# mLSTM cell and leaky-ReLU feed-forward on one core: w_in's row blocks over both partition halves, and row tiles that swap PSUM banks at a drain

## The chip, the core and the metric

The kernel runs on one core of a Trainium2 chip. The core has five engines that work at the same time, each from its own queue of instructions in a fixed order: TensorE (PE in the profile; its weight loads are PEld), VectorE (DVE), ScalarE (ACT), GpSimd (POOL) and SyncE (SP, which here only issues DMAs). Matrix products read SBUF and leave their results in PSUM[...]. The metric is the device time of one execution in microseconds, lower is better; three executions of the kernel before gave 541.49, 541.57 and 542.69.

## The reference

An mLSTM cell runs over 4 batches, 8 heads, 768 time steps and heads of 40; its output, 3072 tokens of 320, goes through a feed-forward layer of width 2048 with a leaky ReLU.

```python
for t in range(S):
    m_new = np.maximum(f_gate[:, :, t] + m, i_gate[:, :, t])
    f_stab = np.exp(f_gate[:, :, t] + m - m_new)
    i_stab = np.exp(i_gate[:, :, t] - m_new)
    C = f_stab * C + i_stab * einsum('bhd,bhe->bhde', v_t, k_t)
    n = f_stab * n + i_stab * k_t
    y_t = sigmoid(o_t) * einsum('bhde,bhe->bhd', C, q_t) / maximum(abs(sum(n * q_t)), 1)
x = y.transpose(0, 2, 1, 3).reshape(3072, 320)
h = x @ w_in                      # 320 x 2048
out = np.maximum(0.01 * h, h) @ w_out   # 2048 x 320
```

All activations are float32. The two weight matrices come as float64; the kernel reads them as 64-bit words and narrows them to float32 itself.

## The kernel before

**Chunks and steps.** The 768 time steps are cut into six chunks of 128. A step s is one batch of one chunk (s = 4 * chunk + batch), so there are 24. The cell's work of a step is two pieces: `u_parts` (the products of keys, queries and values, and the state's increments, L576 and L581) and then `u_plain` (chunk 1, L629) or `u_mix` (chunks 2 to 5, L659), which make x of that step. The texts below call them parts(s), plain(s) and mix(s). Between them `ahead(s + 1)` prepares the next step: copies on ACT, products on DVE, and on POOL the values `vu` (L458), the state (L556) and the mask (L429); for steps up to 7 it also holds `u_split`, transposes on TensorE with four ACT copies after them (L504). The mask's exponentials (L437, ACT) are handed out three per unit of feed-forward work. Chunk 0 has code of its own, `first_chunk`.

**Feed-forward groups.** Group g is the feed-forward work on the 512 tokens of chunk g; it runs while the cell works on chunk g + 1. It has 32 units. Units 0 to 15 are the first product (`ph`, L723) with a relu on ACT (L731): 320 rows of w_in are five row blocks of 64, and a matmul takes one block of 64 rows on one half of the partitions, so that two row tiles of TensorE, r = 0 (partitions 0 to 63) and r = 1 (64 to 127), work side by side. A pair j is two FF tiles of 128, one for each row tile: row tile r always writes PSUM bank `ph[r]`, and each half of the partitions holds all five blocks of its own tiles, in the order `SLOTS[r]`. A pair has ten matmuls of 512 columns, cut into a unit of six and a unit of four, after which two relus empty the two banks. Four banks (`psf`, tag `mm`) hold two pairs, so that one is emptied while the next fills. Group 0 works in halves of 256 columns, ten matmuls to a unit. Units 16 to 31 are the second product (`po`, L758), 4 matmuls each; each is 128 x 128 by 128 x 320.

**x.** The first product reads x transposed, `xT`, as five blocks of 64 rows on either half. In chunks 0 and 1, `u_x` makes it: three transposes to PSUM and five ACT copies (L709 to L713). Later mix(s) writes x to DRAM, and `gather_x` reads it back with four DMAs.

**Weights.** `load_weights(n)` brings w_in's four column blocks (n < 4; ten DMAs of 64 rows x 256 words each, L213) and w_out's eight row blocks (L218). `narrow_weights(n)` turns one into float32, with one ACT operation (L231) and six DVE operations (L233 to L247). Blocks 0 and 1 are narrowed in the first chunk, the other ten step by step in group 0's units: two steps in units up to 9, then three, from 14 on four.

**Order.** TensorE, DVE, ACT and POOL keep the order in which the program calls them; SP's DMAs are placed by the tile framework. The last loop is that order: unit i of the feed-forward, then any cell pieces due after it. In chunk 1 `place` names the units after which the 13 pieces come; in later chunks the nine pieces (eight in the last) are spread evenly over the first 24 units, which puts them after units 2, 5, 7, 10, 13, 15, 18, 21 and 23. The gates of the next chunk follow unit 0 (DVE) and unit 2 (ACT, L294 and L295); its transposes (L310, L315) are one of the nine pieces. When chunk 5 is done, group 5 runs with no cell pieces.

Of the kernel before, what the change touches and what calls it, by code (L numbers as in the profile page):

```python
# [9 lines left out]
F32 = mybir.dt.float32  # L10
U32 = mybir.dt.uint32
U64 = mybir.dt.uint64
AF = mybir.ActivationFunctionType
# [5 lines left out]
def kernel(  # L19
# [26 lines left out]
    nc = tc.nc  # L46
# [22 lines left out]
    SLOTS = ([0, 2, 4, 1, 3], [1, 3, 0, 2, 4])  # L69
    assert NB * P == S and NF * P == FF and NF % 4 == 0 and D <= DP and H == 2 * PR and BH <= P  # L70
    assert KR == DP and KC == 5 and KC * DP == Dm and GT * 4 <= 2048
# [96 lines left out]
    def f_of(r, j):  # L168
        n, e = divmod(j, 2)
        return 4 * n + 2 * r + e  # L170

    def w_row(r, slot, j):
        n, e = divmod(j, 2)
        at = (2 * slot + e) * P
        return w_in[DP * r : DP * (r + 1), n, at : at + P]

    def run_of(r, at):

        ks = SLOTS[r][at:]
        return ks[0], next((i for i in range(1, len(ks)) if ks[i] != ks[i - 1] + 2), len(ks))  # L180
# [7 lines left out]
    def load_weights(n):  # L188
# [20 lines left out]
        if n < QN:  # L209
            src = moe_w_in[:, n * QC : (n + 1) * QC].rearrange("(k p) (r c) -> r p k c", p=DP, r=2)  # L210
            for slot in range(KC):
                for r in range(2):
                    nc.sync.dma_start(  # L213
                        to[DP * r : DP * (r + 1), 2 * P * slot : 2 * P * (slot + 1)], src[r, :, SLOTS[r][slot], :],
                    )
        else:
            rows = moe_w_out[2 * m * P : 2 * (m + 1) * P, :]
            nc.sync.dma_start(to.rearrange("p (a d) -> p a d", d=Dm), rows.rearrange("(a p) d -> p a d", p=P))  # L218
# [464 lines left out]
    def gather_x(s):  # L683

        c, b = divmod(s, B)
        if ("xT", c) not in st:
            st["xT", c] = wk.tile([P, KC, GT], F32, name="xT", bufs=1)
        xT = st["xT", c]
        src = x_dr[s].rearrange("(k p) t -> p k t", p=DP)
        for r in range(2):  # L690
            at = 0
            while at < KC:
                k0, n = run_of(r, at)
                nc.sync.dma_start(xT[DP * r : DP * (r + 1), at : at + n, ts(b, P)], src[:, k0 : k0 + 2 * n - 1 : 2, :])
                at += n

    def u_x(s):

        c, b = divmod(s, B)
        d = st[s]  # L700
        if b == 0:
            st["xT", c] = wk.tile([P, KC, GT], F32, name="xT", bufs=1)
        xT = st["xT", c]
        xt = psc.tile([P, KF + 1, P], F32, name="xt", tag="c")
        for kk in range(KF):
            nc.tensor.transpose(xt[:, kk, :], d["x"][:, ts(kk, P)], ident[:])
        nc.tensor.transpose(xt[:KR, KF, :], d["x"][:, KF * P :], ident[:])
        tok = ts(b, P)
        nc.scalar.copy(xT[:, :KF, tok], xt[:, :KF, :])  # L709
        nc.scalar.copy(xT[:DP, KF + 1 :, tok], xt[DP:, :KF, :])  # L710
        nc.scalar.copy(xT[DP:, KF : 2 * KF, tok], xt[:DP, :KF, :])
        nc.scalar.copy(xT[:DP, KF, tok], xt[:DP, KF, :])
        nc.scalar.copy(xT[DP:, 2 * KF, tok], xt[:DP, KF, :])  # L713
        del st[s]


    def ff_units(g):
        xT = st["xT", g]

        def rows(j, ph, cols, slots):  # L720
            for slot in slots:
                for r in range(2):
                    nc.tensor.matmul(  # L723
                        ph[r][:, cols], lhsT=w_row(r, slot, j), rhs=xT[DP * r : DP * (r + 1), slot, cols],
                        start=(slot == 0), stop=(slot == KC - 1),
                    )

        def relu(j, ph, cols):
            for r in range(2):
                f = f_of(r, j)  # L730
                nc.scalar.activation(acts[:, f, cols], ph[r][:, cols], AF.Prelu, alpha=0.01)  # L731

        def pair(j):
            ph = []

            def first():
                ph.extend(psf.tile([P, GT], F32, name=f"ph{r}", tag="mm") for r in range(2))
                rows(j, ph, slice(0, GT), range(3))

            def second():  # L740
                rows(j, ph, slice(0, GT), range(3, KC))
                relu(j, ph, slice(0, GT))

            return [first, second]

        def half(j, h):
            ph = [psf.tile([P, GT], F32, name=f"ph{r}", tag="mm") for r in range(2)]
            cols = ts(h, GT // 2)
            rows(j, ph, cols, range(KC))
            relu(j, ph, cols)  # L750
# [18 lines left out]
        if g == 0:  # L769

            ins = [(j, h) for j0 in range(0, NF // 2, 2) for h in range(2) for j in (j0, j0 + 1)]
            return [lambda j=j, h=h: half(j, h) for j, h in ins] + [
                lambda n=n, m=m: part(n, m) for m in range(4) for n in range(B)
            ]
        return [u for j in range(NF // 2) for u in pair(j)] + [
# [118 lines left out]
    with tc.manual_schedule(engines={E.PE, E.DVE, E.Activation, E.Pool}):  # L894
# [16 lines left out]
        place = (2, 5, 7, 10, 12, 15, 16, 18, 21, 22, 24, 26, 28)  # L911
        now = (None for n in range(2, QN + NF // 2) for _ in narrow_weights(n))
        for c in range(1, NB + 1):
# [6 lines left out]
            for i in range(n_ff):  # L920
# [16 lines left out]
                upto = sum(p <= i for p in place) if c == 1 else min(n_c, (i + 1) * n_c // (n_ff - 8))  # L937
# [50 lines left out]
```

## Time and profile before

| | us |
|---|---|
| three executions, median (lowest to highest) | 541.57 (541.49 to 542.69) |
| the profiled execution | 542.91 |
| its span, first to last instruction | 541.1 |
| TensorE busy | 523.1 (97%) |
| first product on TensorE (L723), 1120 records | 218.9 |
| second product on TensorE (L758), 768 records | 216.2 |
| VectorE busy | 249.8 (46%) |
| ScalarE busy | 163.3 (30%) |
| GpSimd busy | 120.4 (22%) |
| mean granted clock of TensorE | 0.962 |

A float32 matmul shows as two records. Idle time of an engine that is not the bound costs nothing, and a wait is named by the engine that released it last. The chain of work that ended last lies on TensorE for 86% of the span. The page also has the span in 40 slices of 13.5 us, with the busy share in tenths.

### The profile page before, as it was taken

The page shows a single profiled execution, that of the slowest core. Times are in us where ns is not written, and L with a number is a line of the kernel's source. Part 1 is how long each engine was busy: PE and PEld are TensorE (multiplying, and loading weights), DVE is VectorE, ACT ScalarE, POOL GpSimd, SP SyncE. Part 2 cuts the span into 40 slices and gives each one's busy share as a digit, 9 for nine tenths or more (in the row PEclk, how much of TensorE's full clock was granted, in tenths as well). Part 3 has the DMA queues.
Part 4 walks back from the last instruction along what each step waited for, and adds up shares of the span by engine and source line. Part 5 has one row for each costly group of instructions (what it writes and reads, how often), then busy time and mean ns, then how long its engine had stood idle before and what let it go on. Part 6 is the DMA issues. An engine that isn't in the chain of part 4 may idle for free.

```text
span 541.1 us, 11162 instructions
## 1 busy us (share of the span) xinstructions
PE 523.1 (97%) x4372; PEld 339.3 (63%) x4372; DVE 249.8 (46%) x443; ACT 163.3 (30%) x450; POOL 120.4 (22%) x157
## 2 busy tenths in 40 slices
PE   7989969979999999999999999999999999999997
PEld 7877858756745477645577645567654577644675
DVE  4688896999635536135527135625034532000000
ACT  4566653533433320034220043310043400022100
POOL 4134352252303332103333003423002100000000
PEclk9658988979999999999999999999999999999999
DMA  9976687977525555564655554556531121100000
GB/s 116 165 202 150 158 202 196 185 169 145 129 68 105 124 139 128 135 130 92 128 144 129 143 121 98 129 142 141 123 100 51 50 84 34 42 1 0 13 12 24
DMA packets 166003, 60.18 MB, mean 111 GB/s; under 512 B 129024, under 2 KB 156224, under 8 KB 165952
## 3 DMA queue, kind: packets, MB, share of 16 engines
q1 hardware_dynamic: 165568, 59.35, 49.6%
q8 instruction: 34, 0.56, 0.4%
q10 hardware_dynamic: 384, 0.13, 0.1%
q14 instruction: 17, 0.14, 0.1%
HBM read 52.72 MB, written 6.72 MB: 110 GB/s over the span
## 4 chain that ended last, share of the span: by engine, by line
PE 86%; DVE 6%; DMA 3%; SPq 2%; ACT 1%; issue 1%; POOL 1%; DVEq 0%; POOLq 0%; ACTq 0%
PE ph L723 37%; PE po L758 36%; PE pT L659 3%; PE sd L576 3%; DMA S<-in_v_dram 1%; PE warm L305 1%; PE sd L581 1%; PE pa L604 1%; DMA raw<-in_moe_w_out_dram 1%; PE sc L524 1%; ACT w L437 1%; PE ab L416 1%; POOL vu L458 1%; PE tkq L512 1%; DVE qn L586 1%
## 5 line engine op out<-in xcount | busy, mean ns | idle before, releaser
L723 PE MATMUL ph<-xT,w_in 64*128 64x512 f32 (+1 forms) x1120 | 218.9, 542 | 0.1
L758 PE MATMUL po<-w_out,acts 128*128 128x320 f32 x768 | 216.2, 440 | 0.0
L758 PEld LDWEIGHTS po<-w_out,acts 128*128 128x128 f32 x768 | 145.8, 193 | 60.7 <-issue 4.0
L723 PEld LDWEIGHTS ph<-xT,w_in 64*128 64x128 f32 x1120 | 108.4, 191 | 91.0 <-issue 84.2
L731 ACT ACTIVATE acts<-ph 128x512 f32<-128x512 f32 (+1 forms) x112 | 54.0, 534 | 153.6 <-PE ph L723 153.5
L586 DVE TENSOR_TENSOR qn<-w,sd 64x512 f32<-64x512 f32 x40 | 27.4, 685 | 122.7 <-PE sd L581 87.8
L556 POOL TENSOR_TENSOR S<-S,f 40x336 f32<-40x336 f32 x36 | 28.8, 800 | 181.3 <-PE pT L659 135.9
L437 ACT ACTIVATE w<-w,gT 128x64 f32<-128x64 f32 (+1 forms) x192 | 52.4, 350 | 1.0 <-DVE w L423 1.0
L484 DVE TENSOR_TENSOR qn<-kqT,ea 64x512 f32<-64x512 f32 (+1 forms) x40 | 30.2, 755 | 4.7 <-ACT kqT L504 3.4
L458 POOL TENSOR_TENSOR vu<-S,gT 64x336 f32<-64x336 f32 x36 | 31.4, 871 | 2.7
L673 POOL TENSOR_TENSOR xb<-xb,den 128x320 f32<-128x320 f32 x16 | 11.6, 727 | 88.5 <-DVE xb L670 88.5
L766 ACT COPY y<-po 128x320 f32<-128x320 f32 x12 | 5.1, 425 | 86.7 <-PE po L758 86.7
L766 ACT COPY hn<-po 128x320 f32<-128x320 f32 x12 | 5.1, 425 | 86.3 <-PE po L758 86.3
L576 PEld LDWEIGHTS sd<-kqT 40*64 40x64 f32 x640 | 21.1, 138 | 12.8 <-issue 10.5
L666 DVE STREAM_TRANSPOSE hb<-pT 128x512 f32<-128x512 f32 x16 | 11.5, 717 | 38.1 <-PE pT L659 38.1
L429 POOL TENSOR_TENSOR w<-w,i 128x512 f32<-128x512 f32 x20 | 27.3, 1365 | 7.9 <-ACT acts L731 6.5
L581 PE MATMUL sd<-vu,kn 64*40 64x42 f32 x576 | 21.2, 218 | 4.0 <-POOL vu L458 4.0
L576 PE MATMUL sd<-kqT 40*64 40x64 f32 x640 | 24.2, 225 | 0.4 <-DVE S L560 0.2
L659 PEld LDWEIGHTS pT<-qn,S 128*64 128x64 f32 x512 | 16.2, 138 | 10.5 <-issue 6.9
L581 PEld LDWEIGHTS sd<-vu,kn 64*40 64x40 f32 x576 | 18.6, 114 | 4.2 <-POOL vu L458 4.2
L677 DVE STREAM_TRANSPOSE x<-xb 128x512 f32<-128x512 f32 x16 | 17.7, 1104 | 7.8 <-POOL xb L673 7.8
L478 DVE STREAM_TRANSPOSE kqT<-rb 128x512 f32<-128x512 f32 x32 | 20.6, 680 | 0.0
(123 smaller groups left out, 362.4 us busy)
## 6 DMA issues: line engine op xcount, KB each, us to landing
w<-a_dr SPq DMA_DIRECT2D x40, 128.0 KB
ea<-a_dr SPq DMA_DIRECT2D x40, 128.0 KB
rb<-in_k_dram SPq DMA_DIRECT2D x64, 80.0 KB
rb<-in_q_dram SPq DMA_DIRECT2D x64, 80.0 KB
rb<-in_o_gate_dram SPq DMA_DIRECT2D x64, 80.0 KB
kn<-in_k_dram SPq DMA_DIRECT2D x24, 160.0 KB
raw<-in_moe_w_out_dram SPq DMA_DIRECT2D x6, 640.0 KB
S<-in_v_dram SPq DMA_DIRECT2D x80, 40.0 KB
```

Source lines behind the costliest of these rows:

```text
L429: nc.gpsimd.tensor_tensor(w, w, cm2.unsqueeze(1).to_broadcast([P, H, SL]), op=ALU.add)
L437: yield nc.scalar.activation(w[:, h, :], w[:, h, :], AF.Exp, bias=gT[c][:, 0, bh : bh + 1], scale=1.0)
L458: nc.gpsimd.tensor_tensor(d["vu"][rows], S_v[s % NL][rows, u, :, :, :V1], g[rows].to_broadcast([SL, H, 2, V1]), op=ALU.mult,)
L484: nc.vector.tensor_tensor(mixed(s)[rows, 1 - r], d["kqT"][rows, 1].rearrange("p (h t) -> p h t", t=SL), d["ea"][rows], op=ALU.mult,)
L556: nc.gpsimd.tensor_tensor(new, old, g, op=ALU.mult)
L576: nc.tensor.matmul(bank[1 - u][toks, h, :], lhsT=kqT[rows, 0, ts(h, SL)], rhs=kqT[rows, 1, ts(h, SL)], start=True, stop=True,)
L581: nc.tensor.matmul(dC[u][:, h].rearrange("p k d -> p (k d)"), lhsT=d["k"][toks, h, :D], rhs=d["vu"][toks, h].rearrange("p k d -> p (k d)") ...
L586: nc.vector.tensor_tensor(mixed(s)[toks, u], w[toks], bank[1 - u][toks], op=ALU.mult)
L659: nc.tensor.matmul(pT[DP * r : DP * (r + 1), j * P + u * SL : j * P + (u + 1) * SL], lhsT=S[:, u, h, :], rhs=m[:, u, h, :], start=True, st ...
L723: nc.tensor.matmul(ph[r][:, cols], lhsT=w_row(r, slot, j), rhs=xT[DP * r : DP * (r + 1), slot, cols], start=(slot == 0), stop=(slot == KC ...
L731: nc.scalar.activation(acts[:, f, cols], ph[r][:, cols], AF.Prelu, alpha=0.01)
L758: nc.tensor.matmul(po[n][:], lhsT=acts[:, f, ts(n, P)], rhs=w_out[:, f, :], start=(f == 0), stop=(f == NF - 1),)
```

## The change

w_in is laid out anew: of its five row blocks of 64, blocks 0 and 2 lie on partitions 0 to 63, blocks 1 and 3 on 64 to 127, once for all FF tiles, and block 4 on the upper half for the first two FF tiles of a column block and on the lower for the other two. One DMA brings the first four row blocks, two more bring the fifth: three for a column block, not ten. xT has three places, not five: rows 0 to 127, rows 128 to 255, and the last 64 rows on both halves. `u_x` makes it with four transposes and one ACT copy, `gather_x` with three DMAs.

So one FF tile's sum now takes products from both row tiles, in turn. Four FF tiles make a group of four units and hold four PSUM banks: `head(0)` and `head(1)` open two banks each, with the blocks of one row tile for each bank; then TensorE drains (`nc.tensor.drain()`), and `tail(0)` and `tail(1)` finish them with the row tiles swapped over the banks, each followed by two relus, the later bank first. A head has four matmuls, a tail six. Group 0, in halves of 256 columns, has both heads in one unit and both tails in the next.

The cell's pieces are placed so that they come between heads and tails where they fall in the first product: in chunk 1 three pieces come one unit earlier (4, 6 and 14 for 5, 7 and 15), and in later chunks the list `steady` sets the units 1, 5, 9, 13, 16, 18, 19, 21 and 23.

```diff
@@ -66,9 +66,8 @@
     KF = Dm // P
     KR = Dm - KF * P
     KC = Dm // DP
-    SLOTS = ([0, 2, 4, 1, 3], [1, 3, 0, 2, 4])
     assert NB * P == S and NF * P == FF and NF % 4 == 0 and D <= DP and H == 2 * PR and BH <= P
-    assert KR == DP and KC == 5 and KC * DP == Dm and GT * 4 <= 2048
+    assert KR == DP and KF == 2 and KC * DP == Dm and GT * 4 <= 2048
 
     consts = ctx.enter_context(tc.tile_pool(name="consts", bufs=1))
     gp = ctx.enter_context(tc.tile_pool(name="gates", bufs=1))
@@ -165,19 +164,16 @@
     w_in = consts.tile([P, QN, WC], F32, name="w_in")
     w_out = consts.tile([P, NF, Dm], F32, name="w_out")
 
-    def f_of(r, j):
-        n, e = divmod(j, 2)
-        return 4 * n + 2 * r + e
-
-    def w_row(r, slot, j):
-        n, e = divmod(j, 2)
-        at = (2 * slot + e) * P
-        return w_in[DP * r : DP * (r + 1), n, at : at + P]
-
-    def run_of(r, at):
-
-        ks = SLOTS[r][at:]
-        return ks[0], next((i for i in range(1, len(ks)) if ks[i] != ks[i - 1] + 2), len(ks))
+    def w_tile(f, ch):
+
+        n, e = divmod(f, 4)
+        if ch < 2 * KF:
+            r, slot = ch % 2, ch // 2
+            at = slot * QC + e * P
+        else:
+            r, slot = (1 if e < 2 else 0), KF
+            at = KF * QC + (e % 2) * P
+        return w_in[DP * r : DP * (r + 1), n, at : at + P], r, slot
 
     HW = 2 * Dm
     wide = moe_w_in.dtype == U64
@@ -207,12 +203,12 @@
             raws[n] = (raw, dst)
             to = raw
         if n < QN:
-            src = moe_w_in[:, n * QC : (n + 1) * QC].rearrange("(k p) (r c) -> r p k c", p=DP, r=2)
-            for slot in range(KC):
-                for r in range(2):
-                    nc.sync.dma_start(
-                        to[DP * r : DP * (r + 1), 2 * P * slot : 2 * P * (slot + 1)], src[r, :, SLOTS[r][slot], :],
-                    )
+            src = moe_w_in[:, n * QC : (n + 1) * QC]
+            nc.sync.dma_start(
+                to[:, : KF * QC].rearrange("p (k c) -> p k c", k=KF), src[: KF * P].rearrange("(k p) c -> p k c", p=P),
+            )
+            for r in range(2):
+                nc.sync.dma_start(to[DP * r : DP * (r + 1), KF * QC :], src[KF * P :, ts(1 - r, QC // 2)])
         else:
             rows = moe_w_out[2 * m * P : 2 * (m + 1) * P, :]
             nc.sync.dma_start(to.rearrange("p (a d) -> p a d", d=Dm), rows.rearrange("(a p) d -> p a d", p=P))
@@ -684,70 +680,73 @@
 
         c, b = divmod(s, B)
         if ("xT", c) not in st:
-            st["xT", c] = wk.tile([P, KC, GT], F32, name="xT", bufs=1)
+            st["xT", c] = wk.tile([P, KF + 1, GT], F32, name="xT", bufs=1)
         xT = st["xT", c]
-        src = x_dr[s].rearrange("(k p) t -> p k t", p=DP)
+        tok = ts(b, P)
+        nc.sync.dma_start(xT[:, :KF, tok], x_dr[s, : KF * P].rearrange("(k p) t -> p k t", p=P))
         for r in range(2):
-            at = 0
-            while at < KC:
-                k0, n = run_of(r, at)
-                nc.sync.dma_start(xT[DP * r : DP * (r + 1), at : at + n, ts(b, P)], src[:, k0 : k0 + 2 * n - 1 : 2, :])
-                at += n
+            nc.sync.dma_start(xT[DP * r : DP * (r + 1), KF, tok], x_dr[s, KF * P :])
 
     def u_x(s):
 
         c, b = divmod(s, B)
         d = st[s]
         if b == 0:
-            st["xT", c] = wk.tile([P, KC, GT], F32, name="xT", bufs=1)
+            st["xT", c] = wk.tile([P, KF + 1, GT], F32, name="xT", bufs=1)
         xT = st["xT", c]
         xt = psc.tile([P, KF + 1, P], F32, name="xt", tag="c")
         for kk in range(KF):
             nc.tensor.transpose(xt[:, kk, :], d["x"][:, ts(kk, P)], ident[:])
+        nc.tensor.transpose(xt[:, KF, :], d["x"][:, Dm - P :], ident[:])
         nc.tensor.transpose(xt[:KR, KF, :], d["x"][:, KF * P :], ident[:])
-        tok = ts(b, P)
-        nc.scalar.copy(xT[:, :KF, tok], xt[:, :KF, :])
-        nc.scalar.copy(xT[:DP, KF + 1 :, tok], xt[DP:, :KF, :])
-        nc.scalar.copy(xT[DP:, KF : 2 * KF, tok], xt[:DP, :KF, :])
-        nc.scalar.copy(xT[:DP, KF, tok], xt[:DP, KF, :])
-        nc.scalar.copy(xT[DP:, 2 * KF, tok], xt[:DP, KF, :])
+        nc.scalar.copy(xT[:, :, ts(b, P)], xt[:])
         del st[s]
 
 
     def ff_units(g):
         xT = st["xT", g]
 
-        def rows(j, ph, cols, slots):
-            for slot in slots:
-                for r in range(2):
-                    nc.tensor.matmul(
-                        ph[r][:, cols], lhsT=w_row(r, slot, j), rhs=xT[DP * r : DP * (r + 1), slot, cols],
-                        start=(slot == 0), stop=(slot == KC - 1),
-                    )
-
-        def relu(j, ph, cols):
-            for r in range(2):
-                f = f_of(r, j)
-                nc.scalar.activation(acts[:, f, cols], ph[r][:, cols], AF.Prelu, alpha=0.01)
-
-        def pair(j):
-            ph = []
-
-            def first():
-                ph.extend(psf.tile([P, GT], F32, name=f"ph{r}", tag="mm") for r in range(2))
-                rows(j, ph, slice(0, GT), range(3))
-
-            def second():
-                rows(j, ph, slice(0, GT), range(3, KC))
-                relu(j, ph, slice(0, GT))
-
-            return [first, second]
-
-        def half(j, h):
-            ph = [psf.tile([P, GT], F32, name=f"ph{r}", tag="mm") for r in range(2)]
-            cols = ts(h, GT // 2)
-            rows(j, ph, cols, range(KC))
-            relu(j, ph, cols)
+        def products(ph, cols, what):
+            for f, ch in what:
+                lhsT, r, slot = w_tile(f, ch)
+                first = ch == (0 if f % 4 < 2 else 1)
+                last = ch == (2 * KF if f % 4 < 2 else 2)
+                nc.tensor.matmul(
+                    ph[f][:, cols], lhsT=lhsT, rhs=xT[DP * r : DP * (r + 1), slot, cols], start=first, stop=last,
+                )
+
+        def relu(f, ph, cols):
+            nc.scalar.activation(acts[:, f, cols], ph[f][:, cols], AF.Prelu, alpha=0.01)
+
+        def heads(a, b):
+            return [(a, 0), (b, 1), (a, 2), (b, 3)]
+
+        def tails(a, b):
+            return [(b, 4), (a, 1), (b, 0), (a, 3), (b, 2), (a, 4)]
+
+        def group(n, cols):
+
+            fs = range(4 * n, 4 * n + 4)
+            ab = [(fs[0], fs[2]), (fs[1], fs[3])]
+            ph = {}
+
+            def head(e):
+                for f in ab[e]:
+                    ph[f] = psf.tile([P, GT], F32, name="ph", tag="mm")
+                products(ph, cols, heads(*ab[e]))
+
+            def tail(e):
+                if e == 0:
+                    nc.tensor.drain()
+                products(ph, cols, tails(*ab[e]))
+                for f in reversed(ab[e]):
+                    relu(f, ph, cols)
+
+            return [lambda: head(0), lambda: head(1), lambda: tail(0), lambda: tail(1)]
+
+        def half(n, h):
+            u = group(n, ts(h, GT // 2))
+            return [lambda: (u[0](), u[1]()), lambda: (u[2](), u[3]())]
 
         po = {}
 
@@ -768,11 +767,10 @@
 
         if g == 0:
 
-            ins = [(j, h) for j0 in range(0, NF // 2, 2) for h in range(2) for j in (j0, j0 + 1)]
-            return [lambda j=j, h=h: half(j, h) for j, h in ins] + [
+            return [u for n in range(QN) for h in range(2) for u in half(n, h)] + [
                 lambda n=n, m=m: part(n, m) for m in range(4) for n in range(B)
             ]
-        return [u for j in range(NF // 2) for u in pair(j)] + [
+        return [u for n in range(QN) for u in group(n, slice(0, GT))] + [
             lambda n=n, m=m: part(n, m) for n in range(B) for m in range(4)
         ]
 
@@ -908,7 +906,8 @@
 
         ffs = ffs[2:]
         fetch = {4: (3, 4), 8: (5, 6), 15: (7,)}
-        place = (2, 5, 7, 10, 12, 15, 16, 18, 21, 22, 24, 26, 28)
+        place = (2, 4, 6, 10, 12, 14, 16, 18, 21, 22, 24, 26, 28)
+        steady = (1, 5, 9, 13, 16, 18, 19, 21, 23)
         now = (None for n in range(2, QN + NF // 2) for _ in narrow_weights(n))
         for c in range(1, NB + 1):
             if c > 1:
@@ -934,7 +933,7 @@
                         gates(c + 1)
                     if i == (3 if c == 1 else 2):
                         gates_exp(c + 1)
-                upto = sum(p <= i for p in place) if c == 1 else min(n_c, (i + 1) * n_c // (n_ff - 8))
+                upto = min(n_c, sum(p <= i for p in (place if c == 1 else steady)))
                 while done < upto:
                     fn, s = cells[done]
                     fn(s)
```

## The prediction

> **What bounds the kernel now.** I read the page's busy shares and slices first, then TensorE's waits, then the busy time in stretches, and then the chain and single engines' order of time.
>
> ```profile
> span 541.1 us, 11162 instructions
> PE 523.1 (97%) x4372; PEld 339.3 (63%) x4372; DVE 249.8 (46%) x443; ACT 163.3 (30%) x450; POOL 120.4 (22%) x157
> PE   7989969979999999999999999999999999999997
> PEclk9658988979999999999999999999999999999999
> ```
>
> TensorE (PE) is busy for 97%, and its 18 us of idle time lie in the first quarter, where its granted clock also dips. After that the clock is full and the busy row shows nines: there the time is TensorE's own streaming. So the span has two parts, and they answer to different things.
>
> ```profile
> 60.00:80.00 20.00, 15.66 (x279) 13.29 (x281) 19.50 (x28) 11.22 (x31) 7.07 (x7) 0.96 0.82 189
> 100.00:120.00 20.00, 16.70 (x142) 11.66 (x141) 19.27 (x31) 7.28 (x18) 6.55 (x7) 0.83 0.85 191
> 120.00:140.00 20.00, 19.72 (x164) 14.10 (x163) 19.29 (x29) 6.30 (x20) 5.67 (x6) 1.00 0.70 142
> 160.00:180.00 20.00, 20.00 (x206) 10.03 (x204) 11.31 (x22) 7.25 (x22) 5.81 (x7) 1.00 0.59 126
> ```
>
> The columns after the stretch are PE, weight loads, VectorE (DVE), ACT, POOL, clock, DMA share, GB/s. From 60 to 140 us, with group 0's feed-forward work, DVE is full at 19.3 to 19.5 of 20 us (it narrows the weights), and TensorE waits for what stands behind that queue. From 149 us, DVE is half idle and TensorE full.
>
> ```profile
> PE sd L581 <- POOL vu L458: 4.0, 2, 2.3
> PE tg L310 <- DVE hn L640: 3.3, 1, 3.3
> PE dC L536 <- ACT xT L713: 1.8, 1, 1.8
> ```
>
> These are TensorE's waits: parts(5) waits for POOL, the gate transposes wait for plain(6)'s DVE work, and the first chunk waits for the last of five ACT copies of x. TensorE's order of time shows what a long wait costs after it:
>
> ```profile
> 100.03 4.57 PE L758 MATMUL po<-w_out,acts 128*128 128x320 f32 x16
> 113.36 7.55 PE L758 MATMUL po<-w_out,acts 128*128 128x320 f32 x16
> ```
>
> The same 16 records take 4.57 us, and 7.55 us just after the 3.3 us wait: 3 us more, at a lower clock. The chain gives the steady part's prices:
>
> ```profile
> 237.28 6.21 PE ph L723 x28
> 243.49 1.08 PE pT L659 x32
> 468.77 34.53 PE ph L723 x160
> ```
>
> A matmul is two records. 160 records are 80 matmuls at 0.427 us (two row tiles run side by side) = 34.1 us, plus 0.4. The 28 records would be 5.98 and took 6.21: a run cut off by a cell costs 0.23 us at its end. Runs of the output product pay the same (24 records at 0.267 us are 6.40, the chain has 6.66).
>
> **What the Trainium skill says.** "TensorEngine Tiling (Array Packing)", Key Properties: changing the tiling mode drains TensorE; the trace agrees, with 0.23 us at each change. Its Gotcha 1: different row tiles may not be in one PSUM bank at the same time, and software must order them; before, each row tile kept its bank, so no run shows it. "TensorE: Matmul & The Clock Gate", Part 1: about 3.4 us of idleness brings the clock to half for about as long; the 7.55 us above agree. The same page, Part 2: weight loads are pulled ahead of matmuls in flight, and a matmul has some 166 ns of latency that a stream hides. No page prices a drain on TensorE.
>
> **The change, part by part.**
>
> *Feed-forward matmuls.* 10 per pair of FF tiles before and after, the row tiles still alternate: 0. The order inside four units is now heads (4 matmuls, 1.71 us), heads, drain, tails (6, 2.56 us), tails.
>
> *The drains.* 8 in group 0, 4 in each of five later groups. A bare drain stops weight prefetch and exposes the latency, as a change of mode does: 0.2 us at least by the 0.23 above. The upper bound I set at 0.8 (three such gaps, for a sequencer that starts from empty). I take 0.3. In groups 1 to 4 a cell stands right ahead of every drain; that cell forces a mode change anyway, so the drain adds between 0 and 0.3; I take 0.1. Group 5 runs with no cells, so its 4 drains are bare. Sum: 16 x 0.1 + 4 x 0.3 = 2.8 us, bounds 0.8 to 8.0. Group 0's drains fall where DVE sets the pace, and are covered.
>
> *Cell places in the steady chunks.* Before, nine cells followed units 2, 5, 7, 10, 13, 15, 18, 21, 23, and the one at 15 stood where the FF product changes to the output product anyway: 10 runs. After, 1, 5, 9, 13, 16, 18, 19, 21, 23: 11 runs. Three chunks x 0.23 = 0.7 us; the chunk with eight cells stays at 10. The closest parts-to-mix distance stays two output units (4.3 us), which had no wait before.
>
> *PSUM.* All four banks are now taken by one group. The next group's second heads need the banks of the last tails. In the stretch without cells, ACT's pair of relus starts 0.29 us after the stream's end and lasts 1.09:
>
> ```profile
> 473.29 1.09 ACT L731 ACTIVATE acts<-ph 128x512 f32<-128x512 f32 x2 [4.06 <-PE ph L723]
> ```
>
> So the banks are free after 1.38 us, and the first heads last 1.71: 0.33 of cover. At the start of a chunk the gate exponentials (0.86 us by their starts) and three mask exponentials (0.8) now stand between the two relu pairs: 0.29 + 0.97 + 0.86 + 0.73 = 2.85 us after the first tails, and the second tails end at 2.56 + 0.29 = 2.85. Just covered: 0, at most 0.5 x 3.
>
> *x copies and transposes.* Five ACT copies per u_x (0.37 + 0.37 + 0.36 + 0.26 + 0.26 = 1.62 us) become one of 384 columns, an estimate of 0.5 from the 256-column row; one transpose more on TensorE, 0.1 us each. In the first chunk this removes most of the 1.8 us wait and brings the narrowing of w_in's third block, and ACT's copies for parts(4), about 1.6 us forward; DVE idles for 0.91 and 1.46 us for those two now.
>
> *DMAs.* Each w_in block goes from 10 issues (6.90 us of SP) to 3; four blocks, some 19 us less on the queue ahead of the second chunk's loads. TensorE waited only 0.8 us for such a load. Gathering x goes from 4 DMAs to 3, and has 17 us of output product over it: 0.
>
> *Group 0's chunk.* Here the cells plain(4), parts(5), plain(6) move one unit forward, so DVE does their work ahead of two to four narrowing steps. Compare these two instants:
>
> ```profile
> 111.26 0.16 DVE L595 TENSOR_SCALAR den<-hN 128x8 f32<-128x8 f32 x1
> 127.18 1.40 DVE L586 TENSOR_TENSOR qn<-w,sd 64x512 f32<-64x512 f32 x2
> ```
>
> plain(6)'s DVE work no longer stands behind unit 15's four steps (3.7 us), so the 3.3 us wait of the gate transposes goes, with its 3 us of low clock. But 127.18, where DVE reaches parts(7)'s product, has the same DVE work in front of it in either order, with no DVE gap since 94.65. Only gaps closed earlier bring it forward: 1.7 (ACT copies), 0.6, and some 1.0 of the 1.65 at plain(5) make 3.3 us. plain(7) waits for that product: 129.16 becomes 125.8. TensorE arrives there early now: parts(7) at about 113.7, then three output units of 2.2 us: 120. So a wait of about 6 us is late next, in place of two, and it costs 2.5 us of low clock after it (1.9 and 3.0 followed the two before). From there to group 1's first matmul 19.9 us as before, plus 0.4 for transposes: 125.8 + 19.9 + 0.4 + 2.5 = 148.6 against 149.0: -0.4. Bounds: -4 (no low clock, every gap closed) to +3 (gaps stay, low clock full).
>
> **Sum.** -0.4 + 2.8 + 0.7 = +3.1 us. The profiled execution took 542.91, its span 541.1 with 1.8 around it: 546.0 for such a one. The three runs shown have a median of 541.57, so I forecast 544.7. A measurement here can tell about 0.3%, 1.6 us, from no change.
>
> **Rivals.**
> - *Dear drains.* Next to a cell a drain costs 0.3 and bare 0.8: 8.0 + 0.7 + 0.5 = +9, 550.7. For it: no view shows a drain; against: the mode change has already emptied the array.
> - *The first part wins (the faster side).* If the wait at plain(7) is short because DVE closes all its gaps (5.7 us, with 1.97 of ACT's copies among them), group 1 starts 5 us earlier; with drains free beside cells the steady part gives back 1.9: -3.1, 538.5. It decides once DVE reaches parts(7)'s product before about 122. For it: TensorE loses over 12 us here now to waits and clock. Against: DVE is full, and its work is unchanged.
> - *Even.* The wait ends without a low clock (-2.9) and drains cost 2.8 + 0.7: 542.2, no change.
>
> **Numbers.** Chances: forecast 0.50, dear drains 0.17, first part wins 0.20, even 0.13. The forecast's own range is 543.3 to 548. The range of 540 to 549.5 leaves out most of the faster case and the upper half of the dear one. Faster 0.20, same 0.13, slower 0.67.
>
> **What would show it.** The FF run of 160 records in group 5 grows from 34.5 to about 35.7; a steady chunk from 80.1 to 80.7; group 1's first matmul stands near 148.6; TensorE's longest wait is at plain(7)'s matmuls for DVE; the wait of the gate transposes for DVE is gone; the w_in issues shrink. I am wrong if heads wait for ACT's relus in every group, if group 5 grows by over 3 us, or if group 1 starts before 145.

## The result, and the profile after

| | before | after |
|---|---|---|
| executions, median (lowest to highest) | 542.13 (541.49 to 544.66, 4 runs) | 548.94 (547.5 to 549.82, 4 runs) |
| the profiled execution | 542.91 | 548.88 |
| its span | 541.1 | 547.1 |
| mean granted clock of TensorE | 0.962 | 0.978 |

After against before is 1.0114, with an interval of 1.0074 to 1.0154: slower by about 1.1%. The span of the profiled execution grew by 6.0 us where the sum had 3.1. The page of after, busy shares and slices:

```profile
PE 521.6 (95%) x4380; PEld 337.7 (62%) x4380; DVE 252.1 (46%) x443; ACT 154.7 (28%) x418; POOL 122.5 (22%) x157
PE   7889888997999999999999999999999999999997
PEclk9679989998999999999999999999999999999999
```

TensorE's busy time fell by 1.5 us over the whole span while the span grew by 6.0. That sum hides two opposite changes. From group 1's first matmul to the end of group 5's first product (columns as in the prediction, TensorE's busy time after the comma), first before, then after:

```profile
148.96:503.23 354.27, 354.27 (x2803) 205.94 (x2802) 128.62 (x235) 86.22 (x243) 66.54 (x79) 1.00 0.42 98
148.82:508.97 360.15, 357.05 (x2803) 208.85 (x2803) 128.59 (x235) 86.44 (x243) 66.50 (x79) 1.00 0.41 91
```

The clock is full in both, so the loss here is not throttling. The stretch grew by 5.88 us: 3.10 are idle time in gaps too short for a row of tenths, and 2.78 are longer runs of the same number of records. (The ends of matmul records are modelled, so this split is rough; the growth is not.) In the part ahead of it TensorE is busy for 4.3 us less and idle for 4.1 us more. The starts of the groups on TensorE say where the time went. They are read from its order of time, the first `ph` after the last `po` of the group before:

| us | before | after | difference |
|---|---|---|---|
| start to group 1's first matmul | 148.96 | 148.82 | -0.14 |
| groups 1 to 4, beside the cell (nine, nine, nine and eight pieces) | 80.11, 80.10, 80.11, 79.42 | 81.16, 81.28, 81.28, 80.36 | +1.05, +1.18, +1.17, +0.94 |
| group 5's first product, no cell | 34.53 | 36.07 | +1.54 |
| group 5's output product to the end | 37.9 | 38.1 | +0.26 |

The differences add to 6.0. The chain of waits of after shows what a bare drain looks like, in group 5:

```profile
472.97 3.63 PE ph L714 x16
476.60 0.20 issue
476.81 8.85 PE ph L714 x40
485.66 0.08 issue
```

Before, this was one stretch of 160 records. Now it is cut at each drain; a run of 40 records and the "issue" behind it take 8.93 us, where 40 of the 160 records before took 8.63. The first 16 records and their "issue" take 3.83 for 3.45; over the four drains the growth is 1.54. "issue" is time in which TensorE waited for nothing that the profile records. The weight loads of the same place, in their order of time (start, time from the first to the last, idle time ahead of them):

```profile
475.58 0.19 PEld L714 LDWEIGHTS ph<-xT,w_in 64*128 64x128 f32 x2 [0.24 <-issue]
476.78 0.33 PEld L714 LDWEIGHTS ph<-xT,w_in 64*128 64x128 f32 x4 [1.00 <-issue]
```

Loads normally follow one another with 0.24 us of idle time. Across the drain it is 1.00: the load that would have been fetched under the last matmul is held back until the drain is over. At group 5's other three drains it is 0.90 or 0.91.

Beside the cell, the chain of after in group 2:

```profile
234.65 0.11 PE sd L572 x4
234.77 0.29 issue
235.06 8.85 PE ph L714 x40
243.91 1.08 PE pT L655 x32
244.99 0.12 issue
245.11 8.85 PE ph L714 x40
```

The chain of before goes from a cell piece (`sd` or `pT`) straight to `ph`, with no "issue" line between them (its lines at 243.49 and 244.57 are 1.08 us apart, and the piece lasts 1.08). The drain puts 0.29 us there after parts(s) and 0.12 after mix(s). Over groups 1 to 4 it is 0.12 after every mix(s) and 0.16 to 0.29 after parts(s), most often 0.18.

The waits of TensorE in after (total, times, longest):

```profile
PE hN L625 <- DVE qn L582: 3.6, 2, 3.3
PE ph L714 <- issue: 2.5, 13, 0.3
PE hN L625 <- DVE S L556: 1.9, 2, 0.9
```

The wait of the gate transposes for DVE is gone, and plain(7)'s wait for DVE is the longest. The waits of `ph` for "issue" are not in the list of before. All 13 stand at the start of a tail, where a drain is (the 0.29 us above is one of them); gaps of 0.15 us or less are not in the list.

### The profile page after: what moved, and what is told of

Its sections match the earlier page's. It is cut to its first block, busy times and chain, and to the rows that moved or that the text cites. A ratio compares the mean times of both kernels' runs of the same rounds, so it can differ in the third digit from the quotient of the medians.

```text
span 547.1 us, 11130 instructions
## 1 busy us (share of the span) xinstructions
PE 521.6 (95%) x4380; PEld 337.7 (62%) x4380; DVE 252.1 (46%) x443; ACT 154.7 (28%) x418; POOL 122.5 (22%) x157
## 4 chain that ended last, share of the span: by engine, by line
PE 83%; DVE 7%; DMA 3%; SPq 3%; issue 2%; ACT 1%; POOL 1%; DVEq 0%; POOLq 0%; ACTq 0%
PE ph L714 36%; PE po L757 36%; PE pT L655 3%; PE sd L572 3%; SPq L337 2%; DMA a_dr<-a 1%; PE warm L301 1%; PE sd L577 1%; DVE w_out L243 1%; DMA ea<-a_dr 1%; SPq L391 1%; DVE raw L241 1%; DMA rb<-in_k_dram 1%; PE pa L600 1%; DVE w L419 1%
## 5 line engine op out<-in xcount | busy, mean ns | idle before, releaser
L757 PEld LDWEIGHTS po<-w_out,acts 128*128 128x128 f32 x768 | 143.8, 191 | 61.6 <-issue 4.9
L714 PEld LDWEIGHTS ph<-xT,w_in 64*128 64x128 f32 x1120 | 113.3, 190 | 100.5 <-issue 86.7
L552 POOL TENSOR_TENSOR S<-S,f 40x336 f32<-40x336 f32 x36 | 30.0, 833 | 195.8 <-PE pT L655 151.1
L425 POOL TENSOR_TENSOR w<-w,i 128x512 f32<-128x512 f32 x20 | 28.4, 1418 | 1.3
```

The lines of the kernel that those rows point to most:

```text
L425: nc.gpsimd.tensor_tensor(w, w, cm2.unsqueeze(1).to_broadcast([P, H, SL]), op=ALU.add)
L552: nc.gpsimd.tensor_tensor(new, old, g, op=ALU.mult)
L714: nc.tensor.matmul(ph[f][:, cols], lhsT=lhsT, rhs=xT[DP * r : DP * (r + 1), slot, cols], start=first, stop=last,)
L757: nc.tensor.matmul(po[n][:], lhsT=acts[:, f, ts(n, P)], rhs=w_out[:, f, :], start=(f == 0), stop=(f == NF - 1),)
```

## The experiments

### The drains alone, in the kernel before

The kernel before needs no drain, so one can be put into it and nothing else changes. *e1_bare_drains* puts four into each of groups 1 to 5 where almost none touches a cell piece (19 bare, one beside a piece); *e2_cell_drains* puts 19 right after cell pieces in groups 1 to 4, and none in group 5.

```diff
 e1:          def second():
+                if j % 2 == 0:
+                    nc.tensor.drain()
                 rows(j, ph, slice(0, GT), range(3, KC))
 e2:
+            after_cell = False
 ...
+                if c > 1 and i < n_ff // 2 - 1 and after_cell:
+                    nc.tensor.drain()
+                after_cell = False
                 ffs[i]()
 ...
                     fn(s)
                     done += 1
+                    after_cell = True
```

> The kernel before, with one drain and nothing else added in groups 1 to 5, ahead of the second unit of every other pair: 4 per group, 19 of them with no cell ahead and one beside a cell. The trace of the change has group 5 longer by 1.54 us for four bare drains, 0.385 each. Theory (the drain itself is the price): 19 x 0.385 + 0.22 = +7.5 us, each of chunks 2 to 4 at 80.1 + 1.54 = 81.65 us, group 5's first product at 36.1. Rival (the price is in the swap of the row tiles and in waits for the relus' banks, a drain alone is cheap): under +2 us, chunks below 80.5.

> The kernel before, with a drain added right after each cell that falls inside the first product of groups 1 to 4: 19 drains, all beside a cell. Theory (a drain costs some 0.22 us there, on top of the change of mode): 19 x 0.22 = +4.2 us, a chunk of five such drains at 81.2 us, group 5 as before at 34.5. Rival 1 (the mode change hides it, as the forecast had nearly): 0 to 0.1 each, +0 to 2 us. Rival 2 (a drain costs its full 0.385 anywhere): +7.3 us.

Measured: e1 550.23 us, ratio 1.0138 (1.0095 to 1.0181); groups 1 to 4 take 81.56, 81.66, 81.67 and 80.84, and group 5's first product 35.97 (+1.44, 0.36 for each of four). e2 546.52 us, ratio 1.0074 (1.0051 to 1.0096); groups 81.21, 81.22, 81.22 and 80.25, together 4.2 us more for 19 drains (0.22 each), and group 5 unchanged at 34.53. The chain of e2 in group 2 shows its drain as in after:

```profile
238.61 0.12 PE sd L576 x4
238.73 0.18 issue
238.91 6.32 PE ph L723 x28
```

So a drain costs 0.36 us in a running stream and 0.22 where a cell piece has just changed the mode. It does so in the old layout too, so the new operand order and PSUM use need not be invoked for the loss in groups 1 to 5. No run tested group 0's eight drains on their own.

### The places in the later chunks

*e3_after_even_spread* gives the changed kernel the even spread of before in groups 1 to 4; *e8_after_boundary* moves one place of `steady` to the border of the two products.

```diff
 e3:
-                upto = min(n_c, sum(p <= i for p in (place if c == 1 else steady)))
+                upto = sum(p <= i for p in place) if c == 1 else min(n_c, (i + 1) * n_c // (n_ff - 8))
 e8:
-        steady = (1, 5, 9, 13, 16, 18, 19, 21, 23)
+        steady = (1, 5, 9, 13, 15, 18, 19, 21, 23)
```

> The changed kernel, with the cells of the later chunks spread evenly as before (units 2, 5, 7, 10, 13, 15, 18, 21, 23). Two of four drains in each of chunks 2 to 4 and three of four in chunk 5 lose their cell, and the run that the list adds is gone. Theory: a chunk changes from 4 x 0.22 + 0.23 = 1.1 us over 80.1 to 2 x 0.22 + 2 x 0.385 = 1.2, so 81.3 as now, and chunk 5 gains 0.5: +0.8 us on the changed kernel in all. Rival (the new places cost by waits of their own): chunks come back to 80.3 and the time falls by 3 us or more.

> The changed kernel with one place of the later chunks' list moved from unit 16 to unit 15, the border of the two products. Theory (a run cut inside a product costs 0.23 us): four chunks 0.2 to 0.25 us shorter each (80.9, 81.05, 81.05, 80.1 for 81.16, 81.28, 81.28, 80.36), 0.9 us in all. Rival (what the later chunks lost is the drains alone, at 0.28 each, and the place costs nothing): chunks as in the changed kernel, within 0.05.

Measured: e3 551.67 us, ratio 1.016 (1.0121 to 1.0198); groups 81.26, 81.37, 81.37 and 80.81. Against after that is +0.1 in the nine-piece groups, where two drains become bare (2 x 0.14) but a piece stands at the border again (-0.2), and +0.45 in the eight-piece group, where three become bare. e8 549.89 us, ratio 1.0124 (1.0096 to 1.0152); groups 80.96, 81.08, 81.08 and 80.16, each 0.2 shorter than in after. Both theories' figures came out. The total of 0.8 us is too small for the ratio to separate from after's. A cut that lies on the border of the two products instead of inside one is worth 0.2 us, and the new places are the better ones for this layout because they put the drains beside pieces.

### Group 0's chunk: places and narrowing steps

The first part moved by only 0.14 us, but that is not two zeros. Group 0's first matmul stands at 41.53 us before and at 38.46 in after, and group 0 then takes 107.43 and 110.36 us: one half is 3.07 us shorter and the other 2.93 longer. How much of the first is the change's is not shown; the kernels here that share before's first chunk start group 0 anywhere from 39.21 to 41.53. Four kernels took it apart: the changed kernel with the old places (*e4*), the kernel before with the new places (*e5*), the changed kernel with three narrowing steps in place of four in units from 14 on (*e6*), and the kernel before with both edits (*e7*).

```diff
 e4: -        place = (2, 4, 6, 10, 12, 14, 16, 18, 21, 22, 24, 26, 28)
     +        place = (2, 5, 7, 10, 12, 15, 16, 18, 21, 22, 24, 26, 28)
 e5, e7: the reverse, in the kernel before
 e6, e7:
-                    run(now, 2 if i < 10 else 3 if i < 14 else 4)
+                    run(now, 2 if i < 10 else 3)
```

> The changed kernel, with chunk 1's cells at the units of before (5, 7 and 15 for 4, 6 and 14). Theory (VectorE's queue sets the first part, a cell that moves only moves the wait): the wait of the gate transposes for VectorE comes back, the one at plain(7) shrinks, and group 1's first matmul stays within 1.5 us of 148.9; later chunks as in the changed kernel. Rival (the places are what kept the first part from growing): group 1 starts at 151 or later, +2 us or more.

> The kernel before, with nothing changed but chunk 1's places (4, 6 and 14 for 5, 7 and 15). With the old places in the changed kernel group 1 started 2.4 us later. Theory (the places are worth that in any case; the drains of the changed kernel's group 0 and its x copies decide little): the wait of the gate transposes (3.3 us) goes, one at plain(7) comes, group 1 starts between 146.5 and 148, the time falls by 1 to 2.5 us. Rival (the places help only with heads and tails, where cells meet the drains): group 1 at 149 or later.

> The changed kernel, with three narrowing steps per unit to the end of chunk 1 where it has four from unit 14 on (all weights are still there a few units before their use). VectorE then has five steps, some 4 us, less ahead of parts(7)'s product. Theory (that queue is what plain(7) waits for): the 3.3 and 0.9 us waits at plain(7) go, and with them the low clock after it; group 1 starts at 143.5 to 145.5, total about 4 us under the changed kernel. Rival (VectorE's whole work bounds the chunk, its order does not matter): group 1 stays within 1 us of 148.9.

> The kernel before, with both the new places in chunk 1 and three narrowing steps: no drains, no new layout. Theory: group 1 starts at 143 to 145, all later chunks as before (80.1), so 537 us, ratio 0.991. Rival (the gain of the first part in the changed kernel came from its copies and DMAs): group 1 at 147 or later, ratio above 0.996.

| | us | ratio to before | group 1's first matmul |
|---|---|---|---|
| e4_after_old_place | 551.38 | 1.0159 (1.0117 to 1.0201) | 151.21 |
| e5_before_new_place | 543.79 | 1.0024 (1.0012 to 1.0036) | 151.26 |
| e6_after_three_steps | 551.64 | 1.0154 (1.0126 to 1.0181) | 151.93 |
| e7_before_place_steps | 548.21 | 1.0102 (1.0077 to 1.0126) | 153.17 |

My theory missed in all four: each group 1 starts later than expected. The rivals' figures were met in e4, e5 and e7, in e6 neither. The new places alone cost the kernel before something (ratio above 1 with its interval); the rest of the change with the old places starts group 1 at 151.21; both together start at 148.82. The two parts do not add. In e5 the gate transposes' wait went as forecast, but plain(7) then waited longer for DVE than in after. The waits of TensorE in e5, and then in e4:

```profile
PE hN L629 <- DVE qn L586: 5.1, 1, 5.1
```

```profile
PE sd L577 <- POOL vu L454: 3.4, 2, 1.7
PE hN L625 <- DVE qn L582: 2.6, 1, 2.6
```

In e4, with the old places, the gate transposes' wait came back at only 0.7 us of the 3.3, so the places were not the only thing that removed it. How far these starts can be read is limited: kernels whose second chunk is the same as before's (before, e1, e2 and e12 below) start group 1 at 148.96, 149.53, 149.3 and 147.75, and those that share after's (after, e3 and e8) at 148.82, 149.63 and 148.92. Differences of 2 us are near that spread; e5's ratio is the firmer evidence.

e6 and e7 tried to make room on DVE ahead of plain(7). TensorE's order of time in e6, the stretches behind its longest waits:

```profile
123.50 0.31 PE L625 MATMUL hN<-S,qn 128*64 128x42 f32 x2 [0.17 <-DVE qn L582]
129.72 1.34 PE L757 MATMUL po<-w_out,acts 128*128 128x320 f32 x4 [2.56 <-DVE w_out L243]
141.63 2.13 PE L757 MATMUL po<-w_out,acts 128*128 128x320 f32 x4 [2.15 <-DVE w_out L243]
```

The wait at plain(7) shrank from 3.3 to 0.17 us as meant. But narrowing that is put off is wanted by the output product a few units later: two waits of together 4.7 us for w_out's blocks took its place. In e7 the same two waits are 7.3 us. Work taken from ahead of one wait on a full engine came back as a wait for that work.

### DMAs and copies

*e9_after_many_dmas* brings each w_in block in ten DMAs again; *e10_after_four_copies* makes xT in four ACT copies.

```diff
 e9:
-            nc.sync.dma_start(
-                to[:, : KF * QC].rearrange("p (k c) -> p k c", k=KF), src[: KF * P].rearrange("(k p) c -> p k c", p=P),
-            )
+            for k in range(KF):
+                for r in range(2):
+                    for e in range(2):
+                        nc.sync.dma_start(
+                            to[DP * r : DP * (r + 1), k * QC + e * 2 * P : k * QC + (e + 1) * 2 * P],
+                            src[k * P + DP * r : k * P + DP * (r + 1), ts(e, 2 * P)],
+                        )
 e10:
-        nc.scalar.copy(xT[:, :, ts(b, P)], xt[:])
+        tok = ts(b, P)
+        nc.scalar.copy(xT[:, 0, tok], xt[:, 0, :])
+        nc.scalar.copy(xT[:, 1, tok], xt[:, 1, :])
+        nc.scalar.copy(xT[:DP, KF, tok], xt[:DP, KF, :])
+        nc.scalar.copy(xT[DP:, KF, tok], xt[DP:, KF, :])
```

> The changed kernel, but each column block of w_in comes by ten DMAs again (eight of 64 rows x 256 words for the first four row blocks, two for the fifth) into the new layout. Theory (the number of issues ahead of group 0 has no part in where group 1 starts, since TensorE waited 0.8 us for such a load): group 1's first matmul at 148.8 within 0.7, later chunks as in the changed kernel, ratio within 0.003 of the changed kernel's. Rival (the shorter queue on SP is part of what made up for the drains in the first part): group 1 starts 1.5 us or more later, near 150.5 to 151.

> The changed kernel, but x goes from PSUM to its three places in four ACT copies (1.3 us by the rows of before) in place of one of 0.48. Theory (the one copy is what brings the second chunk's first work forward, by the 1.8 us wait that went): group 1 starts 0.8 to 2 us later, at 149.6 to 150.8; later chunks as in the changed kernel (80 to 81.3). Rival (VectorE is bound by its whole work, and the copy only moved a wait): group 1 at 148.8 within 0.5.

Measured: e9 550.9 us, ratio 1.0148 (1.0119 to 1.0177), group 1 at 149.85: between the two expectations, inside the spread named above, so inconclusive as a time. Its order of time on TensorE does show waits that after does not have, for a load that stands behind the longer queue of issues:

```profile
52.08 0.25 PE L498 MATMUL tk<-ident,rb 64*40 64x64 f32 x2 [1.60 <-DMA rb<-in_q_dram]
68.48 0.25 PE L498 MATMUL tk<-ident,rb 64*40 64x64 f32 x2 [1.29 <-DMA rb<-in_q_dram]
```

None of their 2.9 us reaches the later wait: plain(7) comes at 125.39 in e9 and at 125.73 in after, and has waited 3.3 us in both (the trace puts the end of e9's wait down to a DMA, `ea<-a_dr`). Group 0's first matmul, 1.0 us later in e9 (39.48 for 38.46), is made up for by then too. What makes group 1 later in e9 lies behind it: the 30 and the 8 records after that wait take 1.94 and 4.58 us there, 1.64 and 3.51 in after, that is, 1.4 us more at a low clock after the same wait.

e10 550.67 us, ratio 1.015 (1.0118 to 1.0182), group 1 at 149.31: just inside the rival's 0.5, but 0.5 is also inside the spread named above, so this start does not decide either. The theory's size was wrong for a plain reason. The one copy of after takes 0.48 us, and ACT's order of time in e10 has the four starting within 0.6 us of each other, so the narrowing step behind them starts 0.65 us later (50.29 for 49.64), not 0.8 to 2.

### A version that beats both

If a cut run costs 0.2 us, fewer cuts should pay, in the layout of before and without drains. *e11_joined_cells* had the joined places on top of e7; *e12_before_joined* has them on the kernel before alone.

```diff
+        joined = (2, 6, 6, 10, 10, 15, 15, 15, 19)
-                upto = sum(p <= i for p in place) if c == 1 else min(n_c, (i + 1) * n_c // (n_ff - 8))
+                upto = min(n_c, sum(p <= i for p in (place if c == 1 else joined if n_c == 9 else joined[:6] + joined[7:])))
```

> As the run before (e7), and in the later chunks the cell's pieces are joined: mix(s) directly before parts(s + 1), the gates at the boundary of the two products, at units 2, 6, 6, 10, 10, 15, 15, 15, 19: six runs of feed-forward work per chunk in place of ten. Theory (each cut costs 0.23 us): 4 x 0.23 = 0.9 us less per chunk, minus the changes of mode inside a joined piece; chunks at 79.2 to 79.8, 1.2 to 3.6 us under e7. Rival (joined pieces wait for each other's VectorE and GpSimd work): TensorE's waits return and chunks stand above 80.1.

> The kernel before, its second chunk unchanged; only the later chunks hand out their nine cell pieces at five places of the feed-forward (after units 2, 6, 6, 10, 10, 15, 15, 15, 19) in place of nine. Theory (a cut of a run costs 0.2 to 0.27 us at its end, and nothing else sets these chunks): three or four cuts less, so chunks of 79.3 to 79.6 for 80.1, the one with eight pieces 78.8 to 79.4 for 79.4; group 1 starts at 149.0 to 149.5 as before; 1.5 to 2.5 us less in all, ratio 0.995 to 0.998, faster than both kernels. Rival (joined pieces wait for each other, parts for the copies of ahead): a new wait of TensorE inside the pieces, chunks of 80.1 or more.

Measured: e11 547.73 us, ratio 1.0079 (1.0055 to 1.0102), group 1 at 154.47, groups 79.51, 80.32, 79.51 and 79.45: the later chunks came out as expected but for one, and e7's late first part hid it. e12 540.37 us over 9 runs, ratio 0.9956 (0.9938 to 0.9974), groups 79.52, 80.07, 79.51 and 78.63. They are 2.0 us less than before's in all. Four cuts less a chunk at 0.2 would be 3.2. One chunk gained nothing: its first run of 32 `ph` records took 7.62 us where before's took 7.07, and at that run's start a weight load (227.83) waited 0.27 us for ACT's copy `hn` (L766), a wait that no other chunk of e12 has; why only this one has it is not shown. The other two chunks of nine pieces gained 0.59 each, not 0.8: the three pieces joined at unit 15 take 3.05 us, where apart they took 1.08, 1.08 and 0.68. Group 1 also started 1.2 us earlier, in a second chunk that is the same as before's, so that part of the profiled execution is not the edit's. The chain of e12 shows two pieces one after the other with no gap, in group 2:

```profile
236.04 8.79 PE ph L723 x40
244.82 1.08 PE pT L659 x32
245.91 0.17 PE sd L576
```

mix(s) is followed at once by parts(s + 1): one return to `ph` for two pieces. e12 is faster than both kernels.

## Why the prediction was right in direction and short in size

The forecast of slower held. The median, 548.94, lies outside the forecast's own range of 543.3 to 548 and only 0.6 us inside the wider one of 540 to 549.5; one of the four executions, 549.82, lies outside that too, so that it held is in part luck. The sum was 2.9 us short (6.0 against 3.1). By its steps:

- **Drains beside cells: the mis-sized term.** I took 0.1 for each of 16, "between 0 and 0.3", because the cell forces a mode change anyway. The groups grew by 4.34 us in all; less 0.6 for the extra cut in three of them (0.2 each by e8), 16 drains cost 3.7 us, 0.23 each (1.6 forecast). e2 has 0.22 with nothing else changed. The change of mode did not make the drain free; the chain puts its 0.12 to 0.29 us after the last matmul of the piece. This term is 2.1 of the 2.9 us.
- **Bare drains.** 0.3 forecast, 0.385 in after and 0.36 in e1: 1.54 for 1.2.
- **The rival "dear drains"** had 0.3 beside a cell and 0.8 bare. All drains outside group 0 cost 5.2 us, about halfway between the forecast's 2.8 and that rival's 8.0. The argument against the rival, that the array is already empty, was the faulty one; what kept the sum down is the low price of the bare ones.
- **Extra cut.** 0.23 each forecast, 0.2 each by e8. Runs of 20 and 32 records before (4.49 and 7.07 us in the chain) fit 0.43 us a matmul and 0.19 a run, so the 0.427 of the prediction was a little low and its 0.23 a little high.
- **Group 0's chunk.** -0.4 forecast, -0.14 measured. That the two are so near is luck: both halves were smaller than forecast, and the spread of this start is 0.8 to 1.8 us. DVE reached parts(7)'s product at 125.01, 2.2 us earlier than before and not 3.3; DVE's idle time at plain(5) went from 1.65 only to 1.42, where it was to give 1.0. TensorE came to plain(7) at 122.4 (forecast 120), so it waited 3.3 us, not 6, and the clock it lost afterwards was less. TensorE's order of time in after:

```profile
115.71 6.73 PE L757 MATMUL po<-w_out,acts 128*128 128x320 f32 x24
125.73 0.31 PE L625 MATMUL hN<-S,qn 128*64 128x42 f32 x2 [3.30 <-DVE qn L582]
126.98 1.64 PE L625 MATMUL hN<-S,qn 128*64 128x42 f32 x30 [0.94 <-DVE S L556]
128.55 3.51 PE L757 MATMUL po<-w_out,acts 128*128 128x320 f32 x8
```

  The last 8 records took 3.51 us where they took 2.42 before, and the 30 ahead of them 1.64 for 1.13: 1.6 us of low clock, 2.5 forecast. Plain(7)'s 30 records start 2.2 us earlier than before (126.98 for 129.16), and 1.6 + 0.44 for the four added transposes is given back. The granted clock in stretches, first before, behind the wait of the gate transposes, then after, behind plain(7)'s:

```profile
112.60:119.40 6.80, 6.80 (x17) 4.58 (x17) 6.61 (x8) 0.00 (x0) 5.30 (x5) 0.50 0.67 140
127.40:130.80 3.40, 3.40 (x28) 2.57 (x25) 3.27 (x6) 0.00 (x0) 0.93 (x1) 0.50 0.62 135
```

  The clock, third from the end, is half for 6.8 us in one and for 3.4 in the other, and 1.00 on either side. Half of each, 3.4 and 1.7, is about what was lost, 3.0 and 1.6. The prediction took its 7.55 us as agreeing with a low clock of about 3.4 us; the trace has twice that there, and its 2.5 us lies between the two prices. Its "19.9 us as before" is 19.8 by its own lines (148.96 less 129.16).

  What e4 and e5 add is that "places" and "the rest" may not be separable as the prediction took them, as far as the spread lets one say; why they combine so well stays open.
- **x copy, w_in's issues.** ACT's order of time has the copy at 0.48 us, and 0.5 was my estimate. The DMAs were costed at nothing; e9 shows waits of 1.60 and 1.29 us that the short queue takes away, of which nothing is left at plain(7).
- **PSUM.** (A bank is the place in PSUM that one FF tile's sum fills.) The waits name no relu for a head in groups 1 to 5, as forecast. In group 0 there are two, 1.31 us the longest, within the stretch in which DVE sets the pace.
- **Not in the sum:** 0.26 us between the last matmul and the end of the span. The prediction put all 18 us of TensorE's idle time into the first quarter; 3.1 of them lie here, behind the last matmul.

The rival that was faster failed at its own point: DVE reached parts(7)'s product at 125.01, not before 122.

## What to carry to other kernels

In this kernel a drain on TensorE had a price even right behind a cell piece, which changes the tiling mode, so a scheme that drains per group of tiles must win more than 0.2 us a group elsewhere; here the gain (copies, DMA issues) lay on engines that were not the bound. Where TensorE is full, count the places where its stream is cut: e12 took four out of each later chunk and gained 2.0 us over the four chunks with no other change. In a part that waits for a full engine, moving work ahead of or behind one wait should be expected to move the wait, and is tried rather than summed.

## What the runs showed of the hardware that I had not expected

- A drain on TensorE: 0.36 to 0.385 us in a running stream of 512-column matmuls; 0.22 to 0.23 us directly after a cell piece, where the "issue" in the chain is 0.16 to 0.29 after parts(s) and 0.12 after mix(s).
- Across a bare drain the weight loads stand idle for 0.9 to 1.0 us in place of 0.24, while the matmuls come only 0.36 to 0.385 us later.
- The low clock after an idle time of TensorE is not one price: 3.3 us of waiting brought 6.8 us at half clock in before (at the gate transposes; 3.0 us lost), and at plain(7) 3.4 us in after (1.6 lost) but 6.8 in e9, from 126.1 to 132.9 (3.0 lost: 30 records 1.94 for 1.13, 8 records 4.58 for 2.42). What decides between the two lengths is not shown.
- In a part bound by waits, the new places alone (e5) and the rest of the change alone (e4) each put group 1 about 2.3 us later than before, and both together not at all; the spread of that start between kernels that are the same up to there is 1.8 us in single profiles, so this is not firm.
